# Weight sums of the down projection made in pieces during gate and up and kept in DRAM, in a fused attention and GLU kernel

## The chip, the cores and the metric

The kernel runs on one core of a Trainium2 chip. The metric is the device time of one execution in microseconds (us). Engines are named as the profile names them: PE is TensorE's matrix unit and PEld its weight load, DVE is VectorE, ACT is ScalarE, POOL is GpSimd, SP is the SyncE queue, which issues nearly all of this kernel's DMAs, in program order.

## The reference

The input has 2048 rows of 576 features. A linear attention with 32 heads and a GLU layer of 4608 hidden features are computed from the same input and mixed by a gate per row. Everything is float32.

```
x = A_x
g = sigmoid((x * gate_w).sum(-1, keepdims=True))
q, k, v = split_heads(x @ wqkv)              # 32 heads of 18
phi(t) = where(t > 0, t + 1, exp(t)) + 1e-6
kv = einsum("bhsd,bhse->bhde", phi(k), v);  z = phi(k).sum(s)
a = (phi(q) @ kv / (phi(q) . z + 1e-6)) @ wo
h = gelu(x @ w_gate) * (x @ w_up)            # 576 -> 4608
b = h @ w_down                               # 4608 -> 576
return g * a + (1 - g) * b
```

## The kernel before

Every float32 product is made of three matmuls on operands cut into a high half (a copy rounded to the matmul's type) and a low half (the operand less its high half). On top of that, the GLU's products are done by recursive fast matrix multiplication: gate and up with seven products of blocks instead of eight, and down with 26 products instead of more, listed one a line in a table `DOWN`. The price is sums and differences of blocks before the products.

**Gate and up** fill the span from about 330 to 1067 us. The order is written by hand: 72 chains of seven products, two chains interleaved, are laid out in frames of seven steps (`frame`, `i`), and a dictionary `plan`, filled by `put(frame, i, do)`, says what else is written into the program after each step. A frame takes some 11 us. The next block of gate or up weights is loaded into `wraw` (L858, SP), `weight_sums` makes four sums of it on POOL (L373), and `w_split` cuts them into halves (ACT L868, POOL L869 and L870) one frame before PE needs them (`split_at` at step 0 of every other frame). The sums and differences of h that down needs are made on DVE (L996, L999) as `extras`, and stored to and fetched from DRAM (L1008, L1011, L1014); they lie mostly in frames 1, 2 and 3 of every eight.

**Down** runs from 1067.6 us to the end. Its 26 products are cut into three parts each along the hidden features, which makes 78 units (`unit(u, half)`) of 36 matmuls (L1393): four tiles of nine. The stationary operand is a sum of blocks of h (the left operand), the moving one a sum of blocks of `w_down`, 128x864. For each unit:

- `h_load` fetches the left operand from DRAM into one of four raw buffers (L1230), `h_make` makes its high half on ACT and its low half on DVE (L1237 and L1238 where the sign turns, otherwise L1240 and L1241), three units ahead of the use;
- `weight.fetch` loads blocks of `w_down` (L1187) into one of 15 tiles, 18 later on; `weight.sums` makes the named sums of `DOWN`'s last column, five units ahead, on DVE or POOL (L1198); `w_make` makes the high half on ACT (L1203) and the low one on POOL (L1204), three units ahead;
- after a product's third part, each of four banks is multiplied by the gate and added to an output sum in `acc` by DVE (L1403). Where the next product goes on in the same banks, PE may not write a bank before DVE has read it.

A product's line reads: its parts of h, the name of its weight operand (two digits are a block of `w_down`, a letter is a sum), whether it goes on in the same banks, the outputs that it is added to, and the sums that are made for it:

```
-b0 30 - -10 .
-b2 r c . y=21-31,r=y-30
+b3 21 c +11 .
+a7+b7 y 1 -01 .
```

Every engine works in the order of the program. The body of down, for each `u`, is: first half of the unit, `h_make(u + 3)`, `w_make(u + 3)`, `w_sums(u + 5)`, second half of the unit, then at some `u` the remaining sums of the last chain (`later`).

Of the kernel before, what the change touches and what calls it, by code (L numbers as in the profile page):

```python
# [8 lines left out]
F32 = mybir.dt.float32  # L9
F32R = mybir.dt.float32r  # L10
# [74 lines left out]
"""  # L85


class Product:


# [24 lines left out]
def tile_gated_mix(ctx, tc, xt, xs, xn, wk, wv, wq, wo, wgu, wdn, cst, out):  # L115
# [33 lines left out]
    class Scope:  # L149
        def __init__(self):  # L150
            self.stack = ExitStack()
# [212 lines left out]
    def do(n=1):  # L364
        for _ in range(n):
            todo.popleft()()
            load()
# [778 lines left out]
    def raw_view(v):  # L1146
        return f32(v).rearrange("p (g c) -> p g c", g=3)
# [4 lines left out]
    raw_free = deque([0])  # L1152
    vt = [stage[:, i * 864:(i + 1) * 864] for i in range(5)]

    class Weights:


        def __init__(self):
            self.tasks, self.last, self.at, self.free = [], {}, {}, list(range(15))
            used = {}  # L1160
            for j, (m, c) in enumerate(UNITS):
                d = DOWN[m]
                for name in [x for made in d.made for x in (made[1], made[3], made[0])] + [d.v]:
                    used.setdefault((name, c), []).append(j)
            self.spans = {}
            for (name, c), js in used.items():
                first = prev = js[0]
                for j in js[1:] + [10 ** 6]:
                    if j - prev > 9 and name.isdigit() or j == 10 ** 6:
# [3 lines left out]
            self.fetches = sorted((a, name, c) for (name, c), v in self.spans.items() for a, _ in v if name.isdigit())  # L1173

        def tile(self, name, c):
            return vt[self.at[name, c]]
# [6 lines left out]
        def fetch(self, upto):  # L1183
            while self.fetches and self.fetches[0][0] <= upto:
                _, name, c = self.fetches.pop(0)
                self.at[name, c] = self.free.pop(0)
                nc.sync.dma_start(self.tile(name, c).rearrange("p (g c) -> p g c", g=3),  # L1187
                                  wdn[2 * int(name[0]) + int(name[1])][:, 3 * c:3 * c + 3])

        def sums(self, j):  # L1190
            m, c = UNITS[j]
            for name, x, op, y in DOWN[m].made:
                dead = [k for k in (x, y) if any(b == j for _, b in self.spans[k, c]) and k != DOWN[m].v
                        and not any(k in (q[1], q[3]) for q in DOWN[m].made[DOWN[m].made.index((name, x, op, y)) + 1:])]
                a, b = self.tile(x, c), self.tile(y, c)
                self.at[name, c] = self.at.pop((dead[0], c)) if dead else self.free.pop(0)
                eng = nc.gpsimd if j > 4 and (c == 1 or c == 2 and m % 2) else nc.vector
                eng.tensor_tensor(self.tile(name, c), a, b, OP.add if op == "+" else OP.subtract)  # L1198

        def make(self, j):  # L1200
# [21 lines left out]
    def h_direct(j):  # L1222
        nc.sync.dma_start(f32(hb[j][:, 1]), h_d[UNITS[j][1]][:, UNITS[j][0]])
# [8 lines left out]
    def h_make(j):  # L1232
        if j < len(UNITS):
            h, at = hb[j % 4], raw_of.pop(j, None)
            raw = raw_at[at] if j >= DIRECT else f32(h[:, 1])
            if all(minus for minus, _, _ in DOWN[UNITS[j][0]].parts):
                nc.scalar.activation(h[:, 0], raw, AF.Copy, scale=-1.0)  # L1237
                nc.vector.scalar_tensor_tensor(h[:, 1], raw, -1.0, f32(h[:, 0]), op0=OP.mult, op1=OP.subtract)  # L1238
# [98 lines left out]
    for frame, i, do in ((LAST - 4, 6, lambda: weight.fetch(3)), (LAST - 2, 1, lambda: h_direct(0)),  # L1337
                         (LAST - 1, 0, lambda: h_direct(1)), (LAST - 1, 1, lambda: h_load()),
                         (LAST - 1, 1, lambda: w_make(0)), (LAST - 1, 4, lambda: h_make(0)),
                         (LAST - 1, 5, lambda: w_make(1)), (LAST, 0, lambda: h_direct(2)),  # L1340
                         (LAST, 4, lambda: h_make(1)), (LAST, 3, lambda: w_make(2)),
                         (LAST + 1, 0, lambda: (raw_free.extend((1, 2)), h_load())),
                         (LAST + 1, 6, lambda: (h_make(2), weight.sums(3)))):
        put(frame, i, do)

    FRAME = 1, 7, 5, 3, 6, 2, 4
# [62 lines left out]
    def later():  # L1409
        if late:  # L1410
            for do in late.pop(0):
                do()
            if len(late) == 18 - E_FREE:
                raw_free.append(3)
            if not late:
                weight.free.extend((15, 16, 17))

    weight.fetch(7)
    acc_load(1)
    for u in range(len(UNITS)):  # L1420
        unit(u, 0)
        h_make(u + 3)
        w_make(u + 3)
        if not u:
            w_sums(4)
        w_sums(u + 5)
        unit(u, 1)
        if u in LATER:
            later()
        if u in (5, 12, 20):  # L1430
            acc_load((0, 2, 3)[(5, 12, 20).index(u)])
# [74 lines left out]
```

## Time and profile before

| what | us |
|---|---|
| time, median of 3 runs (lowest, highest) | 1453.37 (1453.27, 1453.78) |
| the profiled execution: its own time | 1452.77 |
| the profiled execution: its span, first to last instruction | 1451.0 |
| busy in the span: PE, PEld | 1437.3, 1281.7 |
| busy in the span: DVE, ACT, POOL | 989.0, 640.8, 823.6 |

The granted TensorE clock is full in all forty slices of the span. Some matmul records can be missing, and ends of matmuls are modelled, so a busy PE says that PE was not seen waiting, not that it was at its peak. Where a row of the trace has `[0.83 <-DVE acc L1403]` behind it, the engine sat idle 0.83 us before that instruction, until DVE's instruction of line 1403 on `acc` was done. `x18` behind a row counts the instructions merged into it. In names, `stage`, `vt` and `f` or `sx` hold weight operands of down, `xo`, `wg` and `wu` are large tiles reused for halves of operands and for raw left operands.

### The profile page before, as it was taken

The page shows a single profiled execution, that of the slowest core. Times are in us where ns is not written, and L with a number is a line of the kernel's source. Part 1 is how long each engine was busy: PE and PEld are TensorE (multiplying, and loading weights), DVE is VectorE, ACT ScalarE, POOL GpSimd, SP SyncE. Part 2 cuts the span into 40 slices and gives each one's busy share as a digit, 9 for nine tenths or more (in the row PEclk, how much of TensorE's full clock was granted, in tenths as well). Part 3 has the DMA queues.
Part 4 walks back from the last instruction along what each step waited for, and adds up shares of the span by engine and source line. Part 5 has one row for each costly group of instructions (what it writes and reads, how often), then busy time and mean ns, then how long its engine had stood idle before and what let it go on. Part 6 is the DMA issues. An engine that isn't in the chain of part 4 may idle for free. (4 is left out here: it accounts for less than half of the span.)

```text
span 1451.0 us, 21113 instructions
## 1 busy us (share of the span) xinstructions
PE 1437.3 (99%) x8096; PEld 1281.7 (88%) x8096; DVE 989.0 (68%) x1115; ACT 640.8 (44%) x863; POOL 823.6 (57%) x511
## 2 busy tenths in 40 slices
PE   9999999999999999999999999999999999999999
PEld 9999899988888888888888888888889999999999
DVE  7887898343745538465374753647478989999794
ACT  7554656443333443333433334433345445444542
POOL 1674543365554545535445454455147968799895
PEclk9999999999999999999999999999999999999999
DMA  7574486663634436344263533535888787767771
GB/s 259 158 210 132 155 266 199 236 234 118 224 119 141 156 127 218 131 160 151 103 210 131 192 134 104 194 131 205 304 286 318 249 318 253 235 229 249 246 240 52
DMA packets 123925, 282.13 MB, mean 194 GB/s; under 512 B 12008, under 2 KB 39208, under 8 KB 122672
## 3 DMA queue, kind: packets, MB, share of 16 engines
q1 hardware_dynamic: 121232, 275.80, 55.7%
q10 hardware_dynamic: 2592, 4.98, 0.9%
q8 instruction: 63, 1.03, 0.3%
q14 instruction: 38, 0.31, 0.1%
HBM read 182.20 MB, written 98.50 MB: 193 GB/s over the span
## 5 line engine op out<-in xcount | busy, mean ns | idle before, releaser
L854 PE MATMUL bank<-xo,wg 128*128 128x512 f32 x1764 | 415.4, 389 | 0.5 <-ACT bank L943 0.5
L854 PE MATMUL bank<-xo,wu 128*128 128x512 f32 x1715 | 403.4, 389 | 0.0
L854 PEld LDWEIGHTS bank<-xo,wg 128*128 128x128 f32 x1764 | 330.8, 188 | 69.6 <-ACT bank L943 0.9
L854 PEld LDWEIGHTS bank<-xo,wu 128*128 128x128 f32 x1715 | 321.8, 188 | 67.0 <-DVE bank L976 0.2
L1393 PE MATMUL bank<-xo 128*128 128x288 f32 x2124 | 285.5, 295 | 5.4 <-DVE acc L1403 5.4
L1393 PEld LDWEIGHTS bank<-xo 128*128 128x128 f32 x2124 | 282.0, 188 | 6.9 <-DVE acc L1403 4.1
L373 POOL TENSOR_TENSOR stage<-stage 128x384 f32<-128x384 f32 x132 | 134.7, 1041 | 164.7 <-DMA stage<-wgu 162.0
L943 ACT ACTIVATE bank<-bank 128x512 f32<-128x512 f32 x139 | 80.9, 582 | 242.4 <-PE bank L854 237.2
L869 POOL TENSOR_TENSOR wg<-stage,wg 128x768 fp32r<-128x768 f32 (+3 forms) x41 | 73.9, 1802 | 126.9 <-ACT wg L868 122.3
L1204 POOL TENSOR_TENSOR xo<-vt,xo 128x864 fp32r<-128x864 f32 x42 | 124.2, 2965 | 27.9 <-ACT xo L1203 26.5
L1204 POOL TENSOR_TENSOR xo<-stage,xo 128x864 fp32r<-128x864 f32 x32 | 96.0, 3005 | 66.2 <-ACT xo L1203 66.2
L869 POOL TENSOR_TENSOR wu<-stage,wu 128x768 fp32r<-128x768 f32 (+2 forms) x36 | 74.0, 2056 | 86.2 <-ACT wu L868 81.9
L976 DVE TENSOR_TENSOR bank<-bank,mid 128x512 f32<-128x512 f32 x36 | 25.1, 697 | 143.2 <-ACT mid L971 143.1
L1393 PE MATMUL bank<-xo,wu 128*128 128x288 f32 x684 | 93.8, 295 | 1.4 <-DVE acc L1403 1.4
L1393 PEld LDWEIGHTS bank<-xo,wu 128*128 128x128 f32 x684 | 91.4, 188 | 1.9 <-DVE acc L1403 1.1
L973 DVE TENSOR_TENSOR f<-bank,mid 128x512 f32<-128x512 f32 x18 | 12.5, 692 | 115.0 <-ACT mid L971 110.8
L971 ACT ACTIVATE mid<-bank 128x512 f32<-128x512 f32 x71 | 42.4, 597 | 101.7 <-PE bank L854 90.3
L781 PEld LDWEIGHTS pair<-kw,p 128*128 128x128 f32 x448 | 60.8, 189 | 1.0
L781 PE MATMUL pair<-kw,p 128*128 128x288 f32 x448 | 61.4, 295 | 0.0
L531 PE MATMUL bank<-xo,qw 128*128 128x512 f32 (+1 forms) x231 | 55.7, 392 | 0.0
L1241 DVE TENSOR_TENSOR xo<-wg,xo 128x1536 fp32r<-128x1536 f32 x18 | 48.9, 2718 | 5.2 <-ACT xo L1240 5.2
L531 PEld LDWEIGHTS bank<-xo,qw 128*128 128x128 f32 (+1 forms) x231 | 41.9, 183 | 10.0
(257 smaller groups left out, 2190.6 us busy)
## 6 DMA issues: line engine op xcount, KB each, us to landing
wg<-h_d SPq DMA_DIRECT2D x41, 768.0 KB, 4.2
stage<-wgu SPq DMA_DIRECT2D x33, 768.0 KB, 5.0
h_d<-sx SPq DMA_DIRECT2D x72, 256.0 KB, 2.7
xo<-h_d SPq DMA_DIRECT2D x23, 768.0 KB, 4.2
h_d<-mid SPq DMA_DIRECT2D x64, 256.0 KB, 3.4
h_d<-e SPq DMA_DIRECT2D x63, 256.0 KB, 4.7
vt<-wdn SPq DMA_DIRECT2D x29, 432.0 KB, 5.2
e<-h_d SPq DMA_DIRECT2D x13, 768.0 KB
```

The source lines that it names most:

```text
L373: nc.gpsimd.tensor_tensor(o, a, b, OP.subtract)
L531: nc.tensor.matmul(ps[:wa.shape[1]], wa, xa, start=(k == 0), stop=(k == len(ops) - 1), skip_group_check=g == 4)
L781: nc.tensor.matmul(y[:, i, :288], p[:, 5 * a + g], KW[g][:, wl, i * 288:(i + 1) * 288], start=(n == 0), stop=(n == 13))
L854: nc.tensor.matmul(ps, w_, x_, start=start and i == 0, stop=i == 6, skip_group_check=not start)
L869: nc.gpsimd.tensor_tensor(w[:, i, 3:5], src[:, :, 0:2], f32(w[:, i, 0:2]), OP.subtract)
L943: nc.scalar.activation(o, src, AF.Copy)
L971: nc.scalar.activation(d_sum, d, AF.Copy)
L973: nc.vector.tensor_tensor(es[3], ps["c"], d_sum, OP.add)
L976: nc.vector.tensor_tensor(d, ps["c"], d_sum, OP.add)
L1204: nc.gpsimd.tensor_tensor(w[:, 1], src, f32(w[:, 0]), OP.subtract)
L1241: nc.vector.tensor_tensor(h[:, 1], raw, f32(h[:, 0]), OP.subtract)
L1393: nc.tensor.matmul(y, h[:, hl, g, t * 128:(t + 1) * 128], w[:, wl, g * 288:(g + 1) * 288], start=first and c == 0 and n == 0, stop=c == NK ...
```

## The change

Nine of the 18 named sums of `DOWN` (`y r v w z o x k m`), those of the first fourteen products, are no longer made in down. They are made during gate and up in nine groups `g` (one for every 512 rows of `w_down`), each of pieces of 128x288, and stored to DRAM tensors `v_d`; down then fetches them like blocks of `w_down`. A group is a table of 26 entries: `0:0<00` loads block 00 into slot 0, `4:2=0+1` adds slots 0 and 1 into slot 2, `5:2>o` stores slot 2 as o; the number ahead is a time, stretched over 31 steps. The steps are those of frames 4 to 64 without frames 1, 2 and 3 of every eight. There are five slots: four in a part of `stage` that is free after frame 3, and a new tile `fifth`. An add goes to POOL at steps 4 to 6 and at step 0 of even frames, else to DVE.

With it come these edits. From n = 3 on, the weight sums of gate and up are written into the program at step 1 of the next frame, where they stood at step 5 right behind the load. Down has 11 weight tiles, 14 later on, in place of 15 and 18. The space goes to two more raw buffers for left operands (`hr`), usable from units 5 and 6 on. The first weight fetch reaches unit 4 where it reached unit 3, and the early calls of `weight.sums(3)` and `w_sums(4)` go.

```diff
+SUMS = """
+0:0<00 0:1<01 0:3<10 4:2=0+1 5:2>o 6:3=0+3 7:3>w 7:0<11 8:4=1+3 8:2<21 9:4>x 9:1<31 11:0=0+4 12:0>k 13:2=2-1
...
+    v_d = {name: dram.tile([128, NF2 // 2, 288], F32, name=f"v_d{name}") for name in "yrvwzoxkm"}
...
+    fifth = stages.tile([128, 320], F32, name="fifth")
...
+        def do(self, what, eng):
+            o, s, g = self.slots[int(what[0])], self.slots, self.g
+            if what[1] == "<":
+                nc.sync.dma_start(o, v_at(what[2:])[:, g])
+            elif what[1] == ">":
+                nc.sync.dma_start(v_at(what[2:])[:, g], o)
+            else:
+                eng.tensor_tensor(o, s[int(what[2])], s[int(what[4])], OP.add if what[3] == "+" else OP.subtract)
...
-            self.tasks, self.last, self.at, self.free = [], {}, {}, list(range(15))
+            self.tasks, self.last, self.at, self.free = [], {}, {}, list(range(11))
...
             for name, x, op, y in DOWN[m].made:
+                if stored(name):
+                    continue
...
-                eng = nc.gpsimd if j > 4 and (c == 1 or c == 2 and m % 2) else nc.vector
+                eng = nc.gpsimd if (c == 1 or c == 2 and m % 2) else nc.vector
...
-        split_at(4 * n - 3, 0, GATE, *ALL)
-        fetch_at(4 * n - 3, 5, n, UP)
-        split_at(4 * n - 1, 0, UP, *ALL)
-        if n < NF2 - 1:
-            fetch_at(4 * n - 1, 5, n + 1, GATE)
+        for m, frame, blocks in ((GATE, 4 * n - 3, (n, UP)), (UP, 4 * n - 1, (n + 1, GATE))):
+            split_at(frame, 0, m, *ALL)
+            if blocks[0] < NF2:
+                put(frame, 5, lambda at=blocks: nc.sync.dma_start(wraw, wgu[at]))
+                put(frame + 1, 1, lambda: weight_sums(wraw, tsum))
+    light = [(frame, i) for frame in range(4, 65) if frame % 8 not in (1, 2, 3) for i in range(7)]
+    for g in range(NF2 // 2):
+        one = Sums(g)
+        for at, what in one.tasks():
+            frame, i = light[31 * g + at * 31 // 25]
+            eng = nc.gpsimd if i > 3 or frame % 2 == 0 == i else nc.vector
+            put(frame, i, lambda one=one, what=what, eng=eng: one.do(what, eng))
...
-    vt += [dp.tile([128, 864], F32, name=f"vt{i}") for i in range(10)]
+    vt += [dp.tile([128, 864], F32, name=f"vt{i}") for i in range(6)]
+    raw_at += [raw_view(dp.tile([128, 1536], F32R, name=f"hr{i}")) for i in range(2)]
...
-        if not u:
-            w_sums(4)
         w_sums(u + 5)
         unit(u, 1)
+        if u in (5, 6):
+            raw_free.append(u - 1)
+            h_load()
```

PE's instructions are the same in the same order. Three places of the other engines follow; each row is the line of its own kernel, engine operation, result and operands, and shape.

DVE at the start of down, before: `wu<-wu` is the low half of unit 2, the rows of 128x864 are weight sums, the rows on `acc` the reads of the first product.

```order
L1238 SCALAR_TENSOR_TENSOR wu<-wu 128x1536
L1198 TENSOR_TENSOR stage<-stage 128x864 x2
L1238 SCALAR_TENSOR_TENSOR xo<-xo 128x1536
L1198 TENSOR_TENSOR vt_8786<-vt_8785,vt_8786 128x864
L1198 TENSOR_TENSOR stage<-vt_8786,stage 128x864
L1238 SCALAR_TENSOR_TENSOR xo<-wg,xo 128x1536
L1403 SCALAR_TENSOR_TENSOR acc<-bank,probe,acc 128x288 x2
```

The same place now, on the same engine:

```order
L1274 SCALAR_TENSOR_TENSOR wu<-wu 128x1536
L1274 SCALAR_TENSOR_TENSOR xo<-xo 128x1536
L1274 SCALAR_TENSOR_TENSOR xo<-wg,xo 128x1536
L1447 SCALAR_TENSOR_TENSOR acc<-bank,probe,acc 128x288 x2
L1274 SCALAR_TENSOR_TENSOR xo<-wg,xo 128x1536
```

The sums have gone from between the low halves, and nothing has taken their place.

POOL in gate and up, before, over one load of weights: the sums of the raw block (128x384) and the cut into low halves of up's weights, then of gate's.

```order
L373 TENSOR_TENSOR stage<-stage 128x384 x4
L869 TENSOR_TENSOR wu<-stage,wu 128x3x256
L870 TENSOR_TENSOR wu<-stage,wu 32x3x128
L869 TENSOR_TENSOR wu<-stage,wu 128x4x256
L870 TENSOR_TENSOR wu<-stage,wu 32x4x128
L373 TENSOR_TENSOR stage<-stage 128x384 x4
```

The same engine in light frames now; the rows of 128x288 are the new adds:

```order
L1187 TENSOR_TENSOR stage<-stage 128x288 x2
L380 TENSOR_TENSOR stage<-stage 128x384 x4
L1187 TENSOR_TENSOR stage<-stage 128x288
L876 TENSOR_TENSOR wu<-stage,wu 128x3x256
L877 TENSOR_TENSOR wu<-stage,wu 32x3x128
L876 TENSOR_TENSOR wu<-stage,wu 128x4x256
L877 TENSOR_TENSOR wu<-stage,wu 32x4x128
L380 TENSOR_TENSOR stage<-stage 128x384 x4
```

Adds stand ahead of the weight sums and between them and the cut.

SP in gate and up, before, around a load of weights (`stage<-wgu`):

```order
L1011 DMA ha_d2y<-f 128x512
L1011 DMA ha_d_115<-sx 128x512
L1011 DMA ha_d_116<-f 128x512
L858 DMA stage<-wgu 128x1536
L1008 DMA h_d_98<-mid 128x512
```

The same piece of the queue now, with the loads of blocks of `w_down` and the stores of finished sums:

```order
L1185 DMA v_dv<-stage 128x288
L1018 DMA ha_d2y<-f 128x512
L1018 DMA ha_d_115<-sx 128x512
L1018 DMA ha_d_116<-f 128x512
L1183 DMA stage<-wdn 128x288 x3
L1348 DMA stage<-wgu 128x1536
L1185 DMA v_do<-stage 128x288
L1185 DMA v_dw<-stage 128x288
L1183 DMA stage<-wdn 128x288 x2
L1015 DMA h_d_98<-mid 128x512
```

The load of weights has new loads and stores ahead of it and behind it, each of which waits in the one queue for what it reads or overwrites.

More of the change, by code (lines that the diff above doesn't have):

```diff
@@ L1153, in tile_gated_mix, with stored, v_at, __init__ @@
     vt = [stage[:, i * 864:(i + 1) * 864] for i in range(5)]
+    def stored(name):
+        return name.isdigit() or name in v_d
+    def v_at(name):
+        return wdn[2 * int(name[0]) + int(name[1])] if name.isdigit() else v_d[name]
+    class Sums:
+        def __init__(self, g):
+            self.g, self.slots = g, [stage[:, c:c + 288] for c in range(3072, 4224, 288)] + [fifth[:, :288]]
+        def tasks(self):
+            for word in SUMS.split():
+                at, what = word.split(":")
+                yield int(at), what
+        def do(self, what, eng):
[6 more added lines that the diff above has]
+                eng.tensor_tensor(o, s[int(what[2])], s[int(what[4])], OP.add if what[3] == "+" else OP.subtract)
     class Weights:
         def __init__(self):
-            self.tasks, self.last, self.at, self.free = [], {}, {}, list(range(15))
+            self.tasks, self.last, self.at, self.free = [], {}, {}, list(range(11))
             used = {}
@@ L1162, in __init__ @@
                 d = DOWN[m]
-                for name in [x for made in d.made for x in (made[1], made[3], made[0])] + [d.v]:
+                for name in [x for made in d.made if not stored(made[0]) for x in (made[1], made[3], made[0])] + [d.v]:
                     used.setdefault((name, c), []).append(j)
@@ L1336, in tile_gated_mix @@
         put(back, j, lambda k=k, src=src: nc.sync.dma_start(src, hx_d[:, k]))
-    for frame, i, do in ((LAST - 4, 6, lambda: weight.fetch(3)), (LAST - 2, 1, lambda: h_direct(0)),
+    for frame, i, do in ((LAST - 4, 6, lambda: weight.fetch(4)), (LAST - 2, 1, lambda: h_direct(0)),
                          (LAST - 1, 0, lambda: h_direct(1)), (LAST - 1, 1, lambda: h_load()),
@@ L1342, in tile_gated_mix @@
                          (LAST + 1, 0, lambda: (raw_free.extend((1, 2)), h_load())),
-                         (LAST + 1, 6, lambda: (h_make(2), weight.sums(3)))):
+                         (LAST + 1, 6, lambda: h_make(2))):
         put(frame, i, do)
@@ L1415, in later @@
             if not late:
-                weight.free.extend((15, 16, 17))
+                weight.free.extend((11, 12, 13))
     weight.fetch(7)
```

8 lines of the change are left out of this document (5 added, 3 removed).

## The prediction

> **What bounds the kernel now.** I read the table of stretches first, then PE's waits, then PE's and DVE's instructions in order of time. One profiled execution is used throughout: span 1451.0 us, time 1452.77 us; the median of the runs shown is 1453.37 us, 0.60 us more, and I add that at the end. About 0.2% (2.9 us) is what a measurement of this kernel can tell from no change.
>
> The stretches of down, and one of gate and up (columns: length, then busy time of PE, PEld, DVE, ACT and POOL, granted clock, DMA share, GB/s):
>
> ```profile
> 1060.00:1100.00 40.00, 36.43 (x251) 34.49 (x251) 34.51 (x24) 17.77 (x20) 21.55 (x9) 1.00 0.76 263
> 1100.00:1200.00 100.00, 97.76 (x733) 97.01 (x733) 91.99 (x58) 50.15 (x48) 78.37 (x26) 1.00 0.86 307
> 1200.00:1300.00 100.00, 98.15 (x740) 97.47 (x739) 97.46 (x62) 46.06 (x40) 85.15 (x29) 1.00 0.70 238
> 1300.00:1447.80 147.80, 147.79 (x1121) 147.47 (x1119) 117.50 (x81) 66.37 (x60) 129.92 (x41) 1.00 0.58 198
> ...
> 400.00:1000.00 600.00, 600.00 (x2649) 496.81 (x2647) 323.62 (x430) 226.58 (x323) 297.41 (x217) 1.00 0.44 151
> ```
>
> PE never stops in gate and up and stops for 0.01 us after 1300. In down it loses 3.57, 2.24 and 1.85 us in the first three stretches, and in the third DVE is 97% busy. So the bound is TensorE's work at full granted clock, and all that a rearrangement off PE can win is these 7.66 us. Who holds PE up, by PE's waits from 1060 on (total, times, longest):
>
> ```profile
> PE bank L1393 <- DVE acc L1403: 6.8, 8, 1.8
> PE bank L854 <- DVE bank L976: 0.9, 1, 0.9
> ```
>
> Eight waits for DVE's reads of finished banks (L1403) into the output sums; the ninth belongs to the last chain of up. In order of time:
>
> ```profile
> 1083.84 2.60 PE L1393 MATMUL bank<-xo 128*128 128x288 f32 x18 [1.84 <-DVE acc L1403]
> 1087.28 12.18 PE L1393 MATMUL bank<-xo 128*128 128x288 f32 x90 [0.83 <-DVE acc L1403]
> ...
> 1157.35 2.61 PE L1393 MATMUL bank<-xo,wu 128*128 128x288 f32 x18 [0.58 <-DVE acc L1403]
> 1160.78 2.65 PE L1393 MATMUL bank<-xo,wu 128*128 128x288 f32 x18 [0.83 <-DVE acc L1403]
> ...
> 1190.61 7.43 PE L1393 MATMUL bank<-xo 128*128 128x288 f32 x54 [0.83 <-DVE acc L1403]
> ...
> 1231.76 2.62 PE L1393 MATMUL bank<-xo 128*128 128x288 f32 x18 [0.32 <-DVE acc L1403]
> 1235.20 2.63 PE L1393 MATMUL bank<-xo 128*128 128x288 f32 x18 [0.81 <-DVE acc L1403]
> ...
> 1293.14 2.64 PE L1393 MATMUL bank<-xo 128*128 128x288 f32 x18 [0.72 <-DVE acc L1403]
> ```
>
> They add up to 6.76 us. The reads are late because DVE works in order and weight sums (L1198) stand ahead of them. Around the first gap:
>
> ```profile
> 1070.08 2.22 DVE L1198 TENSOR_TENSOR stage<-stage 128x864 f32<-128x864 f32 x2
> 1072.21 1.75 DVE L1238 SCALAR_TENSOR_TENSOR xo<-xo 128x1536 fp32r<-128x1536 f32 x1
> 1074.45 2.35 DVE L1198 TENSOR_TENSOR vt<-vt,vt 128x864 f32<-128x864 f32 x1 [0.49 <-DMA vt<-wdn]
> 1076.90 2.83 DVE L1198 TENSOR_TENSOR stage<-vt,stage 128x864 f32<-128x864 f32 x1
> 1079.65 3.62 DVE L1238 SCALAR_TENSOR_TENSOR xo<-wg,xo 128x1536 fp32r<-128x1536 f32 x1
> 1083.19 0.93 DVE L1403 SCALAR_TENSOR_TENSOR acc<-bank,probe,acc 128x288 f32<-128x288 f32 x2
> ```
>
> Two sums hold DVE from 1074.45 to 1079.73, the low half of a left operand (L1238) follows, and the read comes at 1083.19 when PE is waiting; PE goes on 0.65 us after it began.
>
> **What the change removes, and its price.** Nine of the 18 sums per third of the width go: 27 of 54 instructions of 128x864. In units 0 to 39, up to about 1262 us, no sum is left. What they took there (busy time of the sums alone, DVE then POOL, then of everything):
>
> ```profile
> 1067.00:1262.00 195.00, 35.57 (x15) 38.81 (x12) 1.00 0.78 273
> 1262.00:1300.00 38.00, 8.73 (x3) 10.69 (x3) 1.00 0.71 242
> ...
> 1067.00:1262.00 195.00, 188.96 (x1413) 187.21 (x1412) 182.29 (x118) 92.62 (x87) 151.60 (x51) 1.00 0.78 273
> ```
>
> DVE goes from 182.29 to 182.29 - 35.57 = 146.7 us in a stage of some 189 us (195 less its gaps), so from 93% to 78% busy; POOL from 151.60 to 112.8. The 90 matmuls of the row at 1087.28 take 12.18 us, 0.135 each, so a unit of 36 takes 4.8 us, and a bank is complete three quarters of a unit, 3.6 us, before PE needs it again: a DVE that isn't behind makes no gap. The five gaps up to 1190.61 each have a sum or a queue of sums ahead: 1.84 + 0.83 + 0.58 + 0.83 + 0.83 = 4.91 us, all taken as gone. The pair at 1231 (1.13 us) is less clear, since no sum is directly ahead of it:
>
> ```profile
> 1214.15 1.04 DVE L1198 TENSOR_TENSOR stage<-vt,vt 128x864 f32<-128x864 f32 x1
> ...
> 1224.68 3.61 DVE L1238 SCALAR_TENSOR_TENSOR wu<-wg,wu 128x1536 fp32r<-128x1536 f32 x1
> 1228.22 2.55 DVE L999 TENSOR_TENSOR r<-sx,r 128x512 f32<-128x512 f32 x1
> 1230.68 1.78 DVE L1403 SCALAR_TENSOR_TENSOR acc<-bank,gate,acc 128x288 f32<-128x288 f32 x4
> ```
>
> The same sum takes 1.04 us here and 2.83 in the fence above, the same subtraction 1.75 and 3.62: the long ones lie beside POOL work. With POOL less full they shorten too. I take half of the pair, 0.57 us. The gap at 1293.14 (0.72) stays: the sums of units 45 to 48 are made as before. Gain in down: 4.91 + 0.57 = 5.5 us; ends 0 (the reads stay late for another reason) and 7.66 (every gap of the first table). The condition j > 4 and the calls that go concern sums no longer made: nothing.
>
> What is late next at the first read is the landing of the output sums that it adds to:
>
> ```profile
> 1069.64 3.41 SPq L1379 DMA_DIRECT2D acc<-ga_d  x4
> ...
> acc<-ga_d SPq DMA_DIRECT2D x16, 288.0 KB, 6.6
> ```
>
> The last of the four is issued at 1073.05 and lands at about 1079.7; PE needs the first bank at 1083.84 - 1.84 = 1082.0. A read of 0.5 us fits.
>
> On that slowing, the Trainium skill ("SBUF — State Buffer", section "Who interferes with whom") says that a VectorE instruction with two SBUF inputs and a GpSimd instruction that reads SBUF exclude each other, the second waiting for all of the first. The trace agrees in size: 2.83 is 1.04 and 1.8 more. By that rule the adds put into gate and up would cost both engines there, which is the first rival's ground; the sum above doesn't change.
>
> **What it adds in gate and up.** Each of nine groups has 8 loads, 9 adds and 9 stores of 128x288 (147 KB) over about 31 steps of light frames: 39 adds on DVE, 42 on POOL, and 153 DMAs in SP's one queue. From the sum of 1.04 us for 864 columns, an add of 288 is about 0.35 us alone on DVE (an estimate), 2.2 at worst beside POOL, as the difference above shows: 14 to 84 us on an engine that is idle for 276 of 600. POOL: 42 times 0.8 (estimate from the row of 1.0 for 384 columns), 33 us, idle for 303. The DMA share there is 0.44. PE had no wait in those 600 us, not even in the frames that are left free of adds because DVE has more to do there, so I take 0. What could be held up is the split of the next weights, behind the moved weight sums:
>
> ```profile
> 733.50 4.50 POOL L373 TENSOR_TENSOR stage<-stage 128x384 f32<-128x384 f32 x4 [7.04 <-DMA stage<-wgu]
> 741.49 2.40 POOL L869 TENSOR_TENSOR wu<-stage,wu 128x768 fp32r<-128x768 f32 x1 [3.49 <-ACT wu L868]
> 743.97 1.34 POOL L870 TENSOR_TENSOR wu<-stage,wu 32x384 fp32r<-32x384 f32 x1
> ...
> 749.08 1.75 PE L854 MATMUL bank<-xo,wu 128*128 128x512 f32 x7
> ```
>
> POOL is idle 7.04 us before the sums, waiting for the weights' landing, and 3.49 before the split; the split's first half ends at 745.31, 3.77 before PE takes it. So POOL may come 3.49 + 3.77 = 7.3 us late. The sums now stand three steps (4.7 us) later in the program, after the landing on which they wait anyway; this frees POOL for the adds before them and costs nothing. An add or two lie between sums and split: under 2 us each. SP may stand at a store until its add is done, and the weight load behind it; that too comes out of the 7.3.
>
> **Loads in down.** Weight loads of 442 KB issued in units up to 39 go from 28 to 46, plus two loads of left operands (786 KB) drawn forward: 18 x 0.442 + 1.6 = 9.5 MB on 273 GB/s x 195 us = 53.2, so 62.8 MB in 189 us, 332 GB/s. What DMAs reach, in fortieths of 1067 to 1300 (5.8 us each):
>
> ```profile
> GB/s 313 367 93 258 182 257 278 391 388 418 343 264 242 140 213 263 345 389 215 388 175 372 400 259 320 225 180 158 184 254 210 239 243 259 321 266 181 169 201 347
> ```
>
> Four slices in a row make 385. A weight is fetched about five units (24 us) before its use and a left operand now up to six units ahead, so a burst is absorbed. Cost 0; the ends are under the rivals.
>
> **The four lost weight buffers** matter after unit 48, where a fetch may reuse a buffer that POOL's low half of the same unit has just read, and SP waits for POOL. There POOL is the tight engine:
>
> ```profile
> 1385.30 3.58 POOL L1204 TENSOR_TENSOR xo<-vt,xo 128x864 fp32r<-128x864 f32 x1
> ...
> 1390.67 4.91 PE L1393 MATMUL bank<-xo,wu 128*128 128x288 f32 x36
> ```
>
> The low half of unit 66 is ready 1.79 us before PE begins it, the least in down. Its work is as before, and the fetches concerned are for sums three units later, so 0; at worst about 3 us of lateness less 1.8, 1.2 us for one place.
>
> **The sum:** 1452.77 - 5.5 = 1447.3 us in the profiled execution; with the 0.60 us between it and the median, 1447.9.
>
> **Rivals.**
> First, slower: gate and up pay. If SP's stores hold the weight loads back until POOL is more than 7.3 us late, PE stops at each frame that takes new weights. About 17 of 27 such frames are light. At 0.5 us beyond the slack each, 17 x 0.5 = 8.5 us, less 5.5: 1456.4. From 5.5 / 17 = 0.32 us each on, the change isn't worth it. For it: one in-order queue with 153 more DMAs. Against: the 7.04 and 3.49 us of idling. Chance 0.10.
> Second, DMA becomes down's bound: slower or equal. If no more than the 307 GB/s of 1100 to 1200 can be had, 62.8 MB take 205 us instead of 195, 10 more, 1463; at 320 GB/s 196 us, 1454. Against: that row's share is 0.86, so 357 at full share, above 332. Chance 0.08. The Trainium skill ("DMA: Bandwidth & Descriptors", section "Specifications") gives about 358 GB/s as a core's HBM limit; by that rule 332 fits with 7% to spare, and 1100 to 1200 alone, at (30.7 + 6 x 0.442) MB in 97.8 us = 341, nearly fills it. The trace's slice of 418 is above the page's figure.
> Third, the reads stay late behind the low halves and the last chain's sums: half of the gain, 1450.6. For it: the pair at 1231. Against: 15% more idle time on DVE. Chance 0.15.
> Fourth, POOL late at the end: 1449.1 with one such place. Chance 0.05.
>
> **How the numbers follow.** The forecast (1445.7 to 1449.5) has 0.62. Faster by over 0.2%, below 1450.5: that, half of the third and all of the fourth, 0.74. Slower, above 1456.3: most of the first and part of the second, 0.13, counting their milder ends as the same: 0.13 with half of the third. The low end is 1453.37 - 7.66 = 1445.7. The high end, 1452.0, takes in the third, the fourth and the mild half of the second, and leaves out under 2 in 10.
>
> **What would show it.** Right: no wait of PE for the reads before 1230, DVE under 85% busy in 1067 to 1250, sums gone there, gate and up still without an idle PE, the first unit of down at the same time as before, 1067.6. Wrong: PE waiting for ACT's or POOL's split in frames 4 to 8 of eight (first rival); ACT's casts waiting for left operands or weights from DMA (second); reads at the same lateness with a subtraction ahead (third); gaps after 1380 behind POOL's low halves (fourth).

## The result, and the profile after

| what | before | after |
|---|---|---|
| time, median (lowest, highest) of six runs of each, us | 1453.32 (1452.34, 1454.21) | 1445.11 (1443.79, 1447.15) |
| the profiled execution: its time, its span, us | 1452.77, 1451.0 | 1443.79, 1442.0 |

The ratio is 0.9943, with a 95% interval of 0.9931 to 0.9956: 8.2 us faster (6.4 to 10.0). The forecast was 1447.9, with a range down to 1445.7, so the gain came out larger than forecast and the median lies 0.6 us past the end of the range, which is less than the interval's 1.8 us to either side. The profiled execution of after is the quickest of its six. Two executions, one of before (2397 us) and one of a version below (3709 us), were disturbed and stand in no ratio.

Stretches of after, with the columns of the same table of before (length; busy time of PE, PEld, DVE, ACT and POOL; granted clock, DMA share, GB/s):

```profile
400.00:1000.00 600.00, 600.00 (x2649) 496.99 (x2648) 363.97 (x463) 226.42 (x323) 335.35 (x253) 1.00 0.55 183
1060.00:1100.00 40.00, 40.00 (x282) 38.55 (x281) 29.47 (x21) 20.92 (x22) 19.79 (x8) 1.00 0.90 332
1100.00:1200.00 100.00, 100.00 (x761) 100.00 (x760) 76.07 (x55) 49.85 (x47) 61.01 (x22) 1.00 0.93 347
1200.00:1300.00 100.00, 99.27 (x752) 99.01 (x751) 87.11 (x61) 48.09 (x42) 67.97 (x26) 1.00 0.80 288
```

PE loses 0.73 us from 1060 on where it lost 7.66 (0.90 of these in the last chain of up). DVE fell from 92 to 76 us of busy time in 1100 to 1200. DMAs move 347 GB/s there, where 307 went before, and nothing on PE waits for them. In gate and up DVE took up 40 us and POOL 38, and PE still has no gap. PE's waits from 1060 on, after:

```profile
PE bank L1437 <- DVE acc L1447: 0.7, 1, 0.7
```

PE in order of time, after, at the places of the first gaps and of the last one:

```profile
1067.01 9.66 PE L1437 MATMUL bank<-xo 128*128 128x288 f32 x72
1076.50 4.91 PE L1437 MATMUL bank<-xo,wu 128*128 128x288 f32 x36
1081.25 14.40 PE L1437 MATMUL bank<-xo 128*128 128x288 f32 x108
...
1100.23 14.40 PE L1437 MATMUL bank<-xo 128*128 128x288 f32 x108
1114.47 4.91 PE L1437 MATMUL bank<-xo,wu 128*128 128x288 f32 x36
...
1283.88 2.65 PE L1437 MATMUL bank<-xo 128*128 128x288 f32 x18 [0.73 <-DVE acc L1447]
```

And DVE at the first reads, after:

```profile
1069.48 3.61 DVE L1274 SCALAR_TENSOR_TENSOR xo<-xo 128x1536 fp32r<-128x1536 f32 x1
1073.08 1.76 DVE L1274 SCALAR_TENSOR_TENSOR xo<-wg,xo 128x1536 fp32r<-128x1536 f32 x1
1077.89 0.52 DVE L1447 SCALAR_TENSOR_TENSOR acc<-bank,probe,acc 128x288 f32<-128x288 f32 x1 [3.05 <-PE bank L1437]
```

The read that stood at 1083.19 behind two sums is at 1077.89, and DVE waits for PE instead of PE for DVE. Of the eight waits one is left, at 1283.88, the one that the prediction left standing.

**Where the 9.0 us between the two profiled spans came from.** The first unit of down begins at 1067.01 instead of 1067.60 (0.59). From the first to the last matmul of down it is 371.25 us instead of 379.90, 8.65 less, and only 6.03 of that is idle time of PE (6.76 less 0.73). The other 2.62 us lie in the time of the units themselves. The tail behind the last matmul is 0.23 longer. Two rows of before show one part of it:

```profile
1104.07 14.48 PE L1393 MATMUL bank<-xo 128*128 128x288 f32 x108
1118.39 4.94 PE L1393 MATMUL bank<-xo,wu 128*128 128x288 f32 x36
```

From 1104.07 to 1118.39 three units take 14.32 us, 4.774 each. The same three take 14.24 in after (1100.23 to 1114.47), 4.747 each: 132.6 and 131.9 ns a matmul, with no wait in either. Counted over each trace, before has 23 of 77 units at 4.774 and after has two. That the waits set this pace is not shown: three versions below begin down at 4.774, with no wait of down ahead, and one keeps 4.747 behind a wait. The other part is the units that hold a wait. The unit of before that began at 1077.09 ended at 1083.84, 6.75 us for 1.84 of idle time: 0.16 more than idle time and a unit. The next, with 0.83 idle, took 5.91: 0.30 more. Over the seven waits that went, this comes to 1.7 us.

### The profile page after: what moved, and what is told of

The parts are those of the page before. It is cut to its first block, busy times and chain, and to the rows that moved or that the text cites. A ratio compares the mean times of both kernels' runs of the same rounds, so it can differ in the third digit from the quotient of the medians.

```text
span 1442.0 us, 21510 instructions
## 1 busy us (share of the span) xinstructions
PE 1435.1 (100%) x8096; PEld 1281.3 (89%) x8096; DVE 995.8 (69%) x1139; ACT 640.5 (44%) x863; POOL 824.4 (57%) x541
## 5 line engine op out<-in xcount | busy, mean ns | idle before, releaser
L380 POOL TENSOR_TENSOR stage<-stage 128x384 f32<-128x384 f32 x132 | 139.6, 1078 | 173.8 <-DMA stage<-wgu 144.0
L1240 POOL TENSOR_TENSOR xo<-vt,xo 128x864 fp32r<-128x864 f32 x39 | 112.7, 2892 | 51.5 <-ACT xo L1239 48.7
L1240 POOL TENSOR_TENSOR xo<-stage,xo 128x864 fp32r<-128x864 f32 x33 | 93.8, 2843 | 82.9 <-ACT xo L1239 57.0
L313 POOL TENSOR_TENSOR psum_k<-psum_k,e 128x576 f32<-128x576 f32 x14 | 20.6, 1470 | 50.0 <-DVE gate L306 48.5
```

The lines of the kernel that those rows point to most:

```text
L313: (nc.vector if t < 2 else nc.gpsimd).tensor_tensor(psum_k, psum_k, r, OP.add)
L380: nc.gpsimd.tensor_tensor(o, a, b, OP.subtract)
L1240: nc.gpsimd.tensor_tensor(w[:, 1], src, f32(w[:, 0]), OP.subtract)
```

## The experiments

Each run was compared with runs of before on its own chip (medians 1452.86 to 1454.26). The theory at this point: the named sums keep DVE busy, so that its reads come late; a wait costs more than its idle time. A ratio is a version's time over that of before. Rivals are named in each expectation.

**Which part of the change does it.** The changed kernel without the two more raw buffers:

```diff
-        if u in (5, 6):
-            raw_free.append(u - 1)
-            h_load()
```

> The changed kernel with its two new raw buffers for left operands never used, so four are left as before. Theory (the sums gone from DVE in units 0 to 39 are the whole gain): 1445 us as the changed kernel, within 1 us, no PE wait before 1280 in the profile. Rival (loads drawn further ahead brought part of the gain, since DMA runs at 0.93 there): ACT's casts wait for left operands, PE gaps come back, 1447 to 1450.

Measured 1444.51 us (1443.02 to 1446.51), ratio 0.9941 (0.9926 to 0.9956), one gap of 0.71 at the old place. The buffers bring nothing.

The changed kernel with no piece made in gate and up:

```diff
-    for g in range(NF2 // 2):
+    for g in range(0):
...
-        return wdn[2 * int(name[0]) + int(name[1])] if name.isdigit() else v_d[name]
+        return wdn[2 * int(name[0]) + int(name[1])] if name.isdigit() else wdn["yrvwzoxkm".index(name) % 8]
```

> The changed kernel without the nine groups in gate and up (81 adds and 153 DMAs left out); in down, blocks of w_down are fetched where the stored sums were, as many bytes. Theory (gate and up hide all of it): 1445 us, within 1 us of the changed kernel, PE without a wait in 400 to 1000 in both. Rival (they cost something that the gain covers): 1442 to 1444.

Measured 1445.55 us (1444.78 to 1446.37), ratio 0.9947 (0.9932 to 0.9962). Its stretch in gate and up:

```profile
400.00:1000.00 600.00, 600.00 (x2648) 496.82 (x2648) 323.31 (x429) 226.69 (x323) 297.11 (x217) 1.00 0.44 151
```

DVE is back at 323 us, POOL at 297, the DMA share at 0.44, and the time does not change. So 40 us of DVE, 38 of POOL and 32 GB/s are hidden wholly, and the first rival of the prediction is gone.

The changed kernel with the weight sums of gate and up back at their old place:

```diff
-                put(frame + 1, 1, lambda: weight_sums(wraw, tsum))
+                put(frame, 5, lambda: weight_sums(wraw, tsum))
```

> The changed kernel with gate's and up's weight sums at step 5 right behind their load, as before, so that POOL's adds of steps 5 and 6 and of step 0 of the next frame stand behind sums that wait for a DMA. Theory (POOL may come 7.3 us late in gate and up): no PE wait there, 1445 us within 1 us. Rival (the move is what keeps gate and up free): PE waits for weights in 400 to 1000, 1447 us or more.

Measured 1449.36 us (1447.32 to 1451.80), ratio 0.9975 (0.9964 to 0.9986): half of the gain is lost. PE now stops in gate and up, once for 1.45 us; that place on PE, then on DVE, then on POOL:

```profile
986.04 1.90 PE L861 MATMUL bank<-xo,wg 128*128 128x512 f32 x7 [1.45 <-DVE f L980]
```
```profile
973.66 1.45 DVE L1187 TENSOR_TENSOR fifth<-fifth,stage 128x288 f32<-128x288 f32 x1
984.92 0.46 DVE L1187 TENSOR_TENSOR stage<-stage 128x288 f32<-128x288 f32 x1 [9.81 <-POOL stage L1187]
985.30 0.69 DVE L980 TENSOR_TENSOR f<-bank,mid 128x512 f32<-128x512 f32 x1
```
```profile
980.08 4.05 POOL L380 TENSOR_TENSOR stage<-stage 128x384 f32<-128x384 f32 x4 [3.82 <-DMA stage<-wgu]
984.09 0.80 POOL L1187 TENSOR_TENSOR stage<-stage 128x288 f32<-128x288 f32 x1
```

POOL stands at the weight sums until the weights have landed, its add of a piece stands behind them, DVE's next add needs that one and waits 9.81 us, and the read of a bank that PE needs stands behind DVE's add. The rival's time came, by another path than it named: PE waits for DVE's reads, not for weights. PE's waits in 400 to 1000 make 2.45 us (PE 597.55 of 600), and a second one, of 0.57 us at 676.05, has the same chain behind it: DVE's add waits 4.82 us for POOL's, and ACT and then PE wait for the read behind it. Down itself is as short as in other runs, 372.02 us. Held against the trace of after matmul by matmul, PE falls 4.0 us behind in 400 to 1000, all of it at five waits: some 0.3 us at each beyond its idle time. That is about the 4.2 us between the two medians.

**What in down had to go.** Before, with DVE's share of the nine named sums cut to eight of their 864 columns, then the same with POOL's share:

```diff
+                n = 8 if name in "yrvwzoxkm" and eng is nc.vector else 864
-                eng.tensor_tensor(self.tile(name, c), a, b, OP.add if op == "+" else OP.subtract)
+                eng.tensor_tensor(self.tile(name, c)[:, :n], a[:, :n], b[:, :n], OP.add if op == "+" else OP.subtract)
```

> The kernel before, with the 15 sums of the nine names that are DVE's made over 8 of 864 columns (856 are left out), POOL's 12 full; nothing is made in gate and up. Theory: DVE's place in the queue is the cause, so all gaps up to 1190 go and the pair at 1231 nearly, units run at 4.75 us: 1446 us. Rival (POOL's sums, which lengthen DVE's work, are the larger part): half of the gaps stay, 1449 to 1450.

> The kernel before, with POOL's 12 sums of the nine names over 8 of 864 columns and DVE's 15 full. Theory: some of DVE's sums shorten from 2.9 towards 1.0 us, the gaps lose up to half: 1449 to 1451. Rival (POOL's sums are the larger part): 1446.

DVE's narrow: 1446.61 us (1445.82 to 1447.05), ratio 0.9954 (0.9939 to 0.9969). POOL's narrow (the same edit with `nc.gpsimd`): 1445.13 us (1444.46 to 1446.06), ratio 0.9946 (0.9930 to 0.9963). POOL's alone give the whole gain, which the theory had not expected. DVE's leave one wait of 0.67 us, at unit 33, and the units run at 4.774 us from the start of down, not at the 4.75 expected. Groups of the sums in 1067 to 1262 (busy us, mean ns of one), DVE's narrow and then POOL's narrow:

```profile
L1199 DVE TENSOR_TENSOR vt<-vt,stage 128x8 f32<-128x8 f32 x5 | 10.1, 2021 | 0.0
...
L1199 DVE TENSOR_TENSOR stage<-vt,vt 128x8 f32<-128x8 f32 x2 | 0.3, 154 | 0.0
```
```profile
L1199 DVE TENSOR_TENSOR vt<-vt,stage 128x864 f32<-128x864 f32 x5 | 14.6, 2913 | 0.0
...
L1199 POOL TENSOR_TENSOR vt<-vt,stage 128x8 f32<-128x8 f32 x3 | 5.2, 1722 | 0.0
```

Nine of DVE's 15 sums of eight columns take 2.0 us and six take 0.15 to 0.17. Each of the nine ends with an instruction of POOL that had begun before it, eight times a low half (L1205) and once a sum, as here:

```profile
1103.35 3.44 POOL L1205 TENSOR_TENSOR xo<-vt,xo 128x864 fp32r<-128x864 f32 x1
1104.80 2.01 DVE L1199 TENSOR_TENSOR vt<-vt,stage 128x8 f32<-128x8 f32 x1
```

So what the trace of before gave as DVE's time for sums was in good part waiting for POOL, mostly for its low halves, which stay. This is the exclusion that the Trainium skill states ("SBUF — State Buffer", section "Who interferes with whom"), and these rows agree with it. Narrow sums thus test too little, so the next two are not issued at all; the first edit is shown, the second has `nc.gpsimd`:

```diff
+                if name in "yrvwzoxkm" and eng is nc.vector:
+                    continue
```

> The kernel before without the 15 sums of the nine names that are DVE's (an operand stands for the sum), POOL's 12 full; nothing in gate and up. An 8-column sum on DVE still took 2.0 us of waiting for POOL. Theory (either half of the sums is enough, because DVE is only a few per cent over what it can do): no gap before 1280, 1444.5 to 1446 us, as with 8 columns. Rival (what is left in the 8-column kernel, one gap at unit 33 and a slower pitch, was the price of POOL's sums): 1446.6.

> The kernel before without POOL's 12 sums of the nine names, DVE's 15 full. Theory: DVE's low halves and sums shorten by what they waited for POOL, no gap before 1280, 1444 to 1446 us, as with 8 columns on POOL. Rival (8 columns there left POOL work that mattered): under 1444.

DVE's gone: 1445.61 us (1445.31 to 1446.27), ratio 0.9948 (0.9934 to 0.9963). POOL's gone: 1445.31 us (1444.58 to 1446.54), ratio 0.9947 (0.9933 to 0.9961). Stretches of the two:

```profile
1067.00:1262.00 195.00, 194.22 (x1469) 193.82 (x1468) 170.07 (x106) 96.44 (x90) 153.86 (x53) 1.00 0.79 285
```
```profile
1067.00:1262.00 195.00, 195.00 (x1476) 194.72 (x1475) 177.65 (x123) 97.01 (x91) 111.01 (x41) 1.00 0.81 291
```

Without POOL's half no wait is left ahead of unit 45; without DVE's half one of 0.78 us stands at unit 33, against the expectation, and the time is the same within the noise. DVE needed to fall from 182.3 us of busy time only to 178, not to the 151 that the change leaves it (150.63 in the first experiment). The stretch holds more of PE's work in the faster kernels: against PE's busy time DVE's was 96% before, is 91% and 88% in these two, and 77% in after. With POOL's half gone, DVE at the first reads:

```profile
1075.38 2.21 DVE L1200 TENSOR_TENSOR vt<-vt,vt 128x864 f32<-128x864 f32 x1 [0.63 <-DMA vt<-wdn]
1077.69 1.06 DVE L1200 TENSOR_TENSOR stage<-vt,stage 128x864 f32<-128x864 f32 x1
1078.67 1.75 DVE L1240 SCALAR_TENSOR_TENSOR xo<-wg,xo 128x1536 fp32r<-128x1536 f32 x1
1080.34 0.94 DVE L1405 SCALAR_TENSOR_TENSOR acc<-bank,probe,acc 128x288 f32<-128x288 f32 x2
```

Down begins at 1068.40 here. Both sums still stand ahead of the read, but the second takes 1.06 us instead of 2.83 and the low half 1.75 instead of 3.62, and the read comes 11.9 us into down where it came 15.6 (1083.19 less 1067.60). So a sum ahead of the read is not enough to make it late; how long DVE's instructions take, waiting for POOL included, is what differs in these rows. Its busy share alone does not decide either: at 88% a wait is left, at 91% none. Over the stretch its sums as a whole are no shorter without POOL's (36.27 us for 16, 35.57 for 15 before); its low halves are, 2.33 us on the mean for 2.57.

**What a wait of PE costs.** The changed kernel with subtractions of 128x288 on DVE ahead of a read of a finished bank, six of them at unit 2, or at units 2, 17 and 32:

```diff
+        for _ in range(6 if u in (2,) else 0):
+            nc.vector.tensor_tensor(fifth[:, :288], fifth[:, :288], fifth[:, :288], OP.subtract)
```

> The changed kernel with six extra DVE instructions of 128x288 on an unused tile in unit 2, ahead of its last two reads, so that PE waits once, at the second half of unit 3. Theory (a wait of PE costs its idle time, 0.13 to 0.33 us of restart, and 27 ns more in every unit after it, until another wait): a gap of 1 to 3 us in the trace, the unit longer than 4.75 us by the gap and 0.3 us, units of 4.77 us after it; 1445.1 us plus the gap plus 0.3 to 1.4 us. Rival (it costs its idle time and no more, and the 27 ns of the kernel before have another cause): units of 4.75 us on both sides, 1445.1 us plus the gap.

> The same six instructions in units 2, 17 and 32, where the kernel before also waits. Theory: three gaps of 1 to 3 us, each with 0.3 us beyond its idle time, and units that switch between 4.75 and 4.77 us only at waits, so 1 to 2.4 us beyond the idle time in all. Rival: the idle time alone.

One: 1451.24 us (1449.26 to 1452.61), ratio 0.9985 (0.9976 to 0.9994). Three: 1462.54 us (1461.64 to 1465.58), ratio 1.0069 (1.0055 to 1.0084). PE at the wait, one group:

```profile
1081.32 2.54 PE L1437 MATMUL bank<-xo 128*128 128x288 f32 x18
1087.43 14.59 PE L1437 MATMUL bank<-xo 128*128 128x288 f32 x90 [3.57 <-DVE acc L1447]
1101.86 4.94 PE L1437 MATMUL bank<-xo,wu 128*128 128x288 f32 x36
```

The 90 matmuls behind the wait take 14.4 us to the next row's start, 12.0 elsewhere. The record of the granted clock holds 0.5 for 6.83 us from 1085.95 on:

```profile
1085.95:1092.78 6.83, 5.35 (x22) 5.35 (x23) 4.05 (x7) 1.34 (x1) 0.00 (x0) 0.50 0.48 173
```

The two units around the wait take 6.2 us more than two others, for 3.57 of idle time. The wait was longer than the 1 to 3 us expected, and neither theory nor rival had counted on the clock. The three groups (3.53, 3.53 and 3.97 us of waiting) cost 2.7 to 3.0 us each beyond the waiting. So a long wait is paid nearly twice; but the waits of before reached 1.84 us at most, at full clock. Three subtractions were therefore tried:

> As the kernel with one gap, with three extra DVE instructions in place of six, so that the gap is of the size of those of the kernel before (0.5 to 2 us; that of 3.57 us halved the granted clock for 6.8 us). Theory: the clock stays full, the two units after the wait cost 0.2 to 0.5 us beyond the idle time, and units of 4.77 us may follow it up to unit 45: 1446.5 to 1448 us. Rival (idle time alone): 1446 to 1447, units of 4.75 us after it.

Four runs gave 1446.34 to 1447.26 us, ratio 0.9957 (0.9941 to 0.9973); no profile shows the length of the wait. The same kernel again, and with three and four subtractions at all three units:

> The changed kernel with three subtractions of 128x288 on DVE ahead of the first read of unit 2. Six of them took 4.59 us and made PE wait 3.57, so three (2.3 us) should make it wait about 1.3 us. Theory (a wait of PE costs 0.1 to 0.3 us more than its idle time and leaves slower units of 4.774 us behind it, up to 75 x 0.027 = 2.0 us): the two units around the wait take 1.4 to 1.6 us more than two units do, and the time is 1446.5 to 1448.7. Rival (a wait costs its idle time and nothing else): 1.3 us more over the two units, 1446.4, and the pitch is the same ahead of the wait and behind it.

> The same three subtractions at units 2, 17 and 32. By the gaps that six made (3.53, 3.53, 3.97) less three subtractions, gaps of 1.3, 1.3 and 1.7 us, 4.3 together. Theory (0.1 to 0.3 us beyond each, and slower units): 4.3 + 0.6 + 0.5 to 2.0 over the changed kernel's 1445.1, 1450.5 to 1452.0. Rival (idle time only): 1449.4. The granted clock stays full in both.

> Four subtractions at units 2, 17 and 32: gaps of about 2.0, 2.0 and 2.5 us, 6.5 together. Theory (the clock stays full at waits below 3.5 us; each costs 0.1 to 0.3 beyond its idle time): 1445.1 + 6.5 + 0.6 + 0.5 to 2.0 = 1452.7 to 1454.2. Rival (idle time only): 1451.6. Second rival (the clock is halved already behind waits of 2 us, which behind 3.57 us cost 2.7 us more): about 1460, and the clock row falls below 1.00.

One group of three: 1445.95 us (1445.07 to 1446.90), ratio 0.9948 (0.9931 to 0.9964). Three groups of three: 1448.44 us (1446.85 to 1449.16), ratio 0.9962 (0.9947 to 0.9977). Three groups of four: 1459.43 us (1457.31 to 1460.76), ratio 1.0037 (1.0022 to 1.0052). PE at the second group, with three subtractions and then with four:

```profile
1154.70 2.55 PE L1437 MATMUL bank<-xo,wu 128*128 128x288 f32 x18
1157.61 2.65 PE L1437 MATMUL bank<-xo,wu 128*128 128x288 f32 x18 [0.37 <-DVE acc L1447]
1160.10 14.48 PE L1437 MATMUL bank<-xo 128*128 128x288 f32 x108
```
```profile
1157.73 2.55 PE L1437 MATMUL bank<-xo,wu 128*128 128x288 f32 x18
1162.82 4.19 PE L1437 MATMUL bank<-xo,wu 128*128 128x288 f32 x18 [2.55 <-DVE acc L1447]
1166.84 14.47 PE L1437 MATMUL bank<-xo 128*128 128x288 f32 x108
```

Three subtractions made waits of only 0.41, 0.37 and 0.80 us, less than expected (1.3 to 1.7). The unit from 1154.70 to 1160.10 takes 5.40: 0.26 more than 0.37 of idle time and a unit of 4.774. The other two waits show 0.27 and 0.25 more, and the single one 0.26 (5.41 for 0.40 idle). Behind the single wait the units stay at 4.747 up to unit 48; with three, 69 units are at 4.774, 67 more than in after. Down with three is 4.1 us longer than after's: 1.43 of idle time, 0.78 around the waits, and 67 x 0.027 = 1.8 of slower units, which the single wait, of the same length as the first of the three, did not bring. The rival that a wait costs its idle time alone falls by these rows (the medians alone, whose intervals are some 2 us to each side, would not decide it).

With four subtractions the waits are 2.58, 2.55 and 2.98 us, and the second rival holds: 18 matmuls that take 2.65 us take 4.19. Stretches of that kernel:

```profile
1239.00:1245.00 6.00, 5.81 (x24) 5.82 (x25) 3.54 (x6) 1.81 (x2) 0.00 (x0) 0.50 0.41 143
...
1060.00:1262.00 202.00, 193.29 (x1387) 191.04 (x1387) 148.84 (x118) 92.71 (x88) 100.39 (x39) 0.97 0.84 308
```

**Two versions that might beat the change.** The last gap, at unit 45, has the sum `p` on DVE ahead of it. With `p` on POOL:

```diff
-                eng = nc.gpsimd if (c == 1 or c == 2 and m % 2) else nc.vector
+                eng = nc.gpsimd if (c == 1 or c == 2 and m % 2 or name == "p") else nc.vector
```

> The changed kernel with all three parts of the sum p (units 48 to 50) on POOL; one of them stands on DVE ahead of the reads of unit 44, before the last gap. Theory (a DVE sum ahead of the reads makes the gap): the gap of 0.73 us at unit 45 goes, the unit's 1.0 us with it, and 0.8 us more where units stayed at 4.77 us after it; 1443.5 to 1444.5 us. Rival (two long low halves are enough to make the reads late, or POOL comes late by the added sum): no difference from the changed kernel, or slower.

Measured 1447.06 us (1446.47 to 1448.25), ratio 0.9960 (0.9948 to 0.9973). The gap at 45 is gone, and 1.90 us of gaps stand at units 50 and 51 instead; 70 units run at 4.774 here, the first 45 among them. DVE there:

```profile
1308.58 2.90 DVE L1234 TENSOR_TENSOR vt<-f,sx 128x864 f32<-128x864 f32 x1 [3.97 <-POOL xo L1240]
1311.39 0.93 DVE L1447 SCALAR_TENSOR_TENSOR acc<-bank,gate,acc 128x288 f32<-128x288 f32 x2
```

A sum on DVE waits 3.97 us for POOL's low half, since it overwrites a tile that this reads, and the read behind it is late. With that sum on POOL, the extra raw buffers taken out and the three tiles that fit in their place given to the weights:

```diff
-            self.tasks, self.last, self.at, self.free = [], {}, {}, list(range(11))
+            self.tasks, self.last, self.at, self.free = [], {}, {}, list(range(14))
...
-    vt += [dp.tile([128, 864], F32, name=f"vt{i}") for i in range(6)]
-    raw_at += [raw_view(dp.tile([128, 1536], F32R, name=f"hr{i}")) for i in range(2)]
+    vt += [dp.tile([128, 864], F32, name=f"vt{i}") for i in range(9)]
...
-                weight.free.extend((11, 12, 13))
+                weight.free.extend((14, 15, 16))
```

> The changed kernel without the two raw buffers, with their space given back to weight tiles (14, later 17, for 11 and 14), and all of the sum p on POOL. Theory (with 11 tiles a DVE sum had to wait 4.0 us for POOL's reading of the tile that it overwrites; with 14 it doesn't): no PE wait in down at all, 1443.5 to 1444.7 us. Rival (POOL comes late by the added sum): PE or DVE waits for POOL between units 48 and 71, 1445.5 or more.

Measured 1444.61 us (1443.17 to 1445.78), ratio 0.9941 (0.9928 to 0.9954): the gaps at 45, 50 and 51 are gone, a new one of 0.82 stands at unit 57, against the theory, and the time is not to be told from after's.

## Why the prediction was right and wrong

- **The bound, and what was late.** Right: PE's work, and PE waited for DVE's reads. All waits up to 1262 are gone, the wait at unit 45 stays (0.73; 0.72 was said). Why they were late was half right: with POOL's sums alone gone, DVE's still stand ahead of the reads, and the waits go all the same.
- **The price of the waits.** This step failed. The prediction took PE's idle time as all that could be won, and set the low end of its range by it (7.66 us). A wait costs 0.16 to 0.33 us more than its idle time in the units around it (before's seven: 1.7 us together; 0.25 to 0.27 each where short waits were put in). This is shown, and without it 7.66 us is no upper end. Another 0.8 of the 2.62 us between the two traces is the slower pace of more units (21 x 0.027 = 0.6, and 0.2 in the units that held the waits), and that it belongs to the waits is not shown. The medians went past the end by 0.6 us, which their spread alone could give; the traces, not the medians, show that the step was wrong. Behind waits of 2.5 us and more the clock halves as well, but before had none of these.
- **The pair at 1231** was taken at half, 0.57, and went whole: 0.57 more. The third rival, reads late behind low halves, did not occur.
- **The start of down** was forecast unchanged and came 0.59 earlier. The trace of before has one wait of 0.90 at the last chain of up, which after lacks; but the versions of before begin down anywhere from 1067.1 to 1068.4, and those of after from 1065.9 to 1069.0 (1072.1 without the move), so it is not shown that the change did it.
- The sum for the two profiled executions: 5.5 + 0.57 + 2.6 + 0.6 - 0.2 (tail) = 9.1, against 9.0 measured. Of these the 0.6 and 0.8 of the 2.6 can be luck of the two executions. The medians differ by less, 8.2, since the profile of after fell on its quickest run.
- **What the sums cost.** The prediction took 35.57 us off DVE and 38.81 off POOL as two loads. They are one, in part: the two engines wait for each other, and taking away either half ended the waits before unit 45, but for the one of 0.78. Without POOL's sums, DVE at 91% of PE's busy time was enough. The "93% to 78%" compares shares of 195 and of 189 us; of 189 both, it is 96% to 78%.
- **Gate and up at nothing.** Right, and shown by the run without the pieces. The adds took DVE 40 us (14 to 84 was said) and POOL 38 (33). But of the later place of the weight sums it said only that it frees POOL and "costs nothing", with no price for leaving them: at the old place the same adds lose about 4 us. The two longest waits, 2.0 us of idle time, come through DVE's adds waiting for POOL's. The prediction had weighed only POOL's own lateness against 7.3 us, not a third engine waiting for POOL.
- **Loads in down.** Right: 332 GB/s was said for 1067 to 1262, and after moves 335 there. The second rival's limit of 307 is passed; so is 341, said for 1100 to 1200.
- **The lost buffers.** Right as far as after goes: the low half of unit 66 is ready 1.80 us before its use, 1.79 before. The run with `p` on POOL shows where they would cost: 3.97 us of a waiting DVE, gone when the tiles come back.

## What to carry to other kernels

Idle time of the bounding engine was a lower bound of what its waits cost here, not an upper one: compare the length of a unit of work with and without a wait, and of the units behind it. Where two engines slow each other, the busy time of the one holds waiting for the other: hold its rows against the other's instructions at the same time. The cheaper half to take away may be enough. Where a chain of steps passes between two in-order engines, look for an instruction that waits for a DMA ahead of it in either, and place it behind the landing.

## What the hardware showed

- A unit of 36 matmuls runs at 4.747 or at 4.774 us with nothing waiting, and one trace holds both. The change from one to the other came at a wait, or near unit 48, where most traces have a delay of about 0.1 us. Of eight traces with no wait ahead of unit 45, seven hold 4.747 up to there, and five of these run at 4.774 from unit 48 on; the eighth (`p` on POOL) begins at 4.774. Down began at 4.774 also with three groups of six, and at 4.747 with three of four. What sets it is open; 77 x 0.027 = 2.1 us may be much of the spread of 3.4 us between the runs of after, which was not traced.
- The clock halves behind waits of PE of 2.55 us and more, and not behind 1.84 us or less. Its stretches in the record are multiples of 3.413 us (3.41 and 6.83 at half clock, 71.68 between two), also where it begins 1.4 us after PE went on. There, with four subtractions, PE was idle from 1084.31 to 1086.89 and half clock began at 1088.33: 1.97 us of the idle time lie in the 3.41 us ahead of it. The other stretches of half clock have 2.1 us or more there. This fits fixed windows that count idle time, about 2 us being enough; that it is so is not tested. The Trainium skill ("TensorE: Matmul & The Clock Gate", section "HAM oscillation — how this bites in real kernels") warns of gaps over about 3.4 us; here 2.55 was enough, and the measurement decides.
- Three subtractions ahead of the first read took DVE 1.43 us and four took 3.60: the fourth alone cost 2.2 us. Its row lies with a low half of POOL, as with the sums above:

  ```profile
  1083.96 2.13 POOL L1240 TENSOR_TENSOR xo<-vt,xo 128x864 fp32r<-128x864 f32 x1 [2.70 <-ACT xo L1239]
  1084.26 2.14 DVE L1470 TENSOR_TENSOR fifth<-fifth 128x288 f32<-128x288 f32 x1
  ```

  The other three take 0.44 to 0.46 us each.
